# A list scheduler that counts the delay between dependent VectorE and ScalarE operations, in a fused gated-convolution forward and backward kernel

## The chip, the cores and the metric

The kernel runs on one core of a Trainium2 chip. The metric is the device time of one launch in microseconds, and a version's time is the median of its runs. The engines are TensorE (PE in the profile; PEld are its weight loads), VectorE (DVE), ScalarE (ACT), GpSimd (POOL) and SyncE (SP), which issues most of the DMAs.

## The reference, cut to what matters

The reference computes one output and nine gradients of a layer on x of shape 2048 x 512 in bf16:

```python
xn = layernorm(x)
# branch A: a short causal filter, a gate, a long causal convolution by FFT, a gate
k_shift = sum(k_pad[:, t:t+S, :] * shift_k[:, 3-t] for t in range(4))
kv = k_shift * v
y  = irfft(rfft(pad(kv)) * rfft(pad(ssm_k)))[:S] + kv * ssm_D
s  = xn * y
# branch B: gated linear unit, F = 1376
h = sigmoid(xn @ w_gate) * (xn @ w_up)
g = silu(h @ w_down)
out = x + s * g
# then the gradients of out for x, k, v, shift_k, ssm_k, ssm_D, w_gate, w_up, w_down, given grad_out
```

## The kernel before

The 2048 rows are 16 tiles of 128. The long convolution is done with matrix products against sine and cosine tables that the kernel makes itself at its start, in four channel groups of 128. The work has these stages.

*Start* (`gen_fft_consts`, `k_t`, `f_ln`, `f_xt`). Integer products of two index vectors are made (`m`), shifted into range, and turned by ScalarE's Sin into the table `Cf`; smaller tables `TB` follow. The first convolution kernel `KT` gets `ssm_D` added to its first column and is transposed on TensorE. Four small matmuls spread the short filter `skr` over the partitions, and ScalarE copies them to `skb`. The first tiles of x are normalised: `bn_stats`, `bn_aggr`, then GpSimd's power for 1/sqrt (`f_ln`), and are transposed (`f_xt`), on TensorE or by a DMA. POS is a tile's place in the order in which the tiles are taken.

*Forward* (streams `strG`, `strK`, `strV`, `strX`, interleaved). `strG` computes gate and up projections for nine tiles (`f_gen`). `strK`, `strV` and `strX` take the convolution through its steps `step1`, `flip`, `step3`, `inv3`, `inv1`. Nearly every matmul group is emptied from PSUM by ScalarE or VectorE.

*Backward* (`stepB`). For each tile: `z_gen` (down projection, silu and its derivative), `d_gen` (gradients of gate and up), `x_gen` (gradient of x through both projections and the LayerNorm). The remaining tiles' `f_gen` run in between, and from its later part the weight gradients `dW`.

*Convolution's backward* (`frontC`, `backC`, with `dW` in between), then the rest of `dW` and the drain.

The functions don't emit instructions. `Rec` records every operation with the operations it depends on, in program order (number `n`). `Rec.order` then plays the whole program through a list of costs (`cost`, `dcost`), engine by engine, and `emit` writes the instructions in the order so found; therefore nearly all instructions carry one line number, that of `emit`. In `order`, `free[e]` is the time at which engine `e` is free, `soon[e]` holds operations whose inputs have a known ready time, and `now[e]` those that are ready; of `now[e]` the one with the lowest `n` is taken. `either` holds PSUM evictions that ScalarE or VectorE may do. An operation whose input comes from the same engine counts as ready at once when the one before it has issued: `r = t + occ`, where `t` is the start and `occ` the time that the engine is held. `fin` is the time at which the result is there, some 0.085 us after `t + occ` on VectorE and 0.11 us on ScalarE. PSUM slots are given out in the same pass (`slot`), so the order also settles which eviction a matmul group waits for.

In `x_gen`, `dxn` is the gradient of the normalised x, `sm` holds two row sums, and the result is `u1 = xn * sm[3] + (dxn * r + sm[2])`, to which the direct gradient `goj` is added before it is stored.

Of the kernel before, what the change touches and what calls it, by code (L numbers as in the profile page):

```python
# [8 lines left out]
ACT = mybir.ActivationFunctionType  # L9
ALU = mybir.AluOpType  # L10
# [6 lines left out]
P = 128  # L17
# [153 lines left out]
class Rec:  # L171
# [176 lines left out]
    def order(self):  # L348
# [55 lines left out]
        while ndone < len(ops):  # L404
            best = None
            for e in self.ENGS:
                while soon[e] and soon[e][0][0] <= free[e]:
                    heapq.heappush(now[e], heapq.heappop(soon[e])[1])
                c = None
                if now[e]:  # L410
                    c = (free[e], now[e][0], e, 0)
                elif soon[e]:
                    c = (soon[e][0][0], soon[e][0][1], e, 0)
                if either and e in ("scalar", "vector"):
                    o = min(either, key=lambda o: (max(o.ready, free[e]), o.n))
                    s = (max(o.ready, free[e]), o.n, e, 1)
                    late = free["scalar"] - s[0]
                    if e == "scalar" or late > (0.4 if c is None or c[0] > s[0] + 0.6 else 1.6):
                        if c is None or s[:2] < c[:2]:
                            c = s  # L420
                if c is not None and (best is None or c[:2] < best[:2]):
                    best = c
            if best is None:
                raise RuntimeError("the order is stuck: " + str({k: len(v) for k, v in blocked.items()}))
            t, n, e, shared = best
            op = ops[n]
            if shared:
                either.remove(op)
            else:
                heapq.heappop(now[e] if now[e] else soon[e])  # L430
            q = 1 if shared and e == "vector" else 0
            new = [v for v in op.tiles if v.bank is None]
            if new:
                got = slot(new[0].kind)
                if got is None:
                    blocked[new[0].kind].append(op)
                    continue
                if got[0] > t:
                    op.ready = got[0]
                    push(op)  # L440
                    continue
                new[0].bank = got[1][0]
                for b in got[1]:
                    owner[b] = new[0]
            alt = op.alts[q]
            d = 0.0
            if op.dma:
                occ, d = self.dcost(alt)
                me, other = ("gpsimd", "hw") if e == "gpsimd" else ("hw", "gpsimd")
                t = max(t, pipe[me] - 12.0)  # L450
                t0 = max(pipe[me], t + 1.5)
                share = min(d, max(0.0, pipe[other] - t0))
                pipe[me] = t0 + d + share
                if share:
                    pipe[other] += share
                fin = pipe[me] + (DSL if t > 6 else 1.0)
            else:
                occ, lat = self.cost(alt)
                if e == "scalar" and alt[1] == "activation":
                    f = {ACT.Sin: "sin", ACT.Sigmoid: "sig"}.get(alt[2][2])  # L460
                    if f and f != table:
                        table = f
                        occ, lat = occ + 1.28, lat + 1.28
                fin = t + lat
            free[e] = t + occ
            op.done, op.fin, op.eng = True, fin, e
            seq.append((op, q, t, occ, d))
            ndone += 1
            while lo < len(ops) and ops[lo].done:
                lo += 1  # L470
            while held and held[0] <= lo + LOOK:
                o = ops[heapq.heappop(held)]
                o.ready = max(o.ready, t)
                push(o)
            for v in op.tiles:
                v.left -= 1
                v.last = max(v.last, fin)
                if v.left == 0:
                    for b in range(8):
                        if owner[b] is v:  # L480
                            owner[b] = None
                            banks[b] = v.last + 0.05 + PSL
                    for kind, lst in blocked.items():
                        for o in lst:
                            o.ready = max(o.ready, 0.0)
                            push(o)
                        lst.clear()
            for s in op.succ:
                if s < 0:
                    o = ops[~s]  # L490
                    o.wait -= 1
                    if o.wait == 0:
                        push(o)
                    continue
                o = ops[s]
                if (e == "tensor" and o.alts[0][0] == "tensor") or (e == o.alts[0][0] and len(o.alts) == 1 and not op.dma):
                    r = t + occ
                else:
                    r = fin + 0.045 + (PSL if o.alts[0][0] == "tensor" and not op.dma else 0.0)
                o.ready = max(o.ready, r)  # L500
                o.wait -= 1
                if o.wait == 0:
                    push(o)
# [38 lines left out]
def gen_fft_consts(nc, ar, negpi, Cf, TB):  # L542
# [14 lines left out]
    m = tmp([4, 4, 128], i32)  # L557
    mc = tmp([4, 2, 4, 128], i32)
    for h in range(4):
        eng = nc.gpsimd if h > 0 else nc.vector  # L560
        eng.tensor_tensor(out=m[:, h], in0=a[:, 4 * h:4 * h + 4, None].to_broadcast([P, 4, 128]),
                          in1=b[:, None, :].to_broadcast([P, 4, 128]), op=ALU.mult)
    for h in range(4):
        js = slice(4 * h, 4 * h + 4)
        if h > 1:
            yield
        nc.vector.tensor_scalar(mc[:, h, 1], m[:, h], 19, 19, ALU.logical_shift_left, ALU.arith_shift_right)
        nc.scalar.activation(Cf[:, 1, js], mc[:, h, 1], ACT.Sin, scale=-sc)
        nc.vector.scalar_tensor_tensor(mc[:, h, 0], mc[:, h, 1], -1, mc[:, h, 1], ALU.mult, ALU.max)
        nc.scalar.activation(Cf[:, 0, js], mc[:, h, 0], ACT.Sin, bias=negpi[:, 1:2], scale=-sc)  # L570
# [58 lines left out]
def kernel_impl(ctx, tc, A_q, A_k, A_v, A_shift_k, A_ssm_k, A_ssm_D, B_x, B_w_gate, B_w_up, B_w_down,  # L629
                grad_out, out_0, out_1, out_2, out_3, out_4, out_5, out_6, out_7, out_8, out_9):  # L630
    nc = tc.nc
# [81 lines left out]
        nc.scalar.activation(xnA[:, i, :], xj, ACT.Identity, bias=nmr_all[:, i:i + 1], scale=rstd_all[:, i:i + 1])  # L713

    def f_xt(i):
        if POS[i] > 1 and not 8 < POS[i] < 12:
            T[i]["xnT"] = xnT_r.next()
            nc.sync.dma_start_transpose(T[i]["xnT"], xnA[:, i, :])
            return
        pt = ps_tr([4, 128], name="ps_xnT")  # L720
        for db in range(4):
            nc.tensor.transpose(pt[:, db, :], xnA[:, i, db * 128:(db + 1) * 128], ident)
        T[i]["xnT"] = xnT_r.next()
        nc.evac(T[i]["xnT"], pt[:], 512)
# [125 lines left out]
    consts = gen_fft_consts(nc, ar, negpi, Cf, TB)  # L850
    next(consts)
    make_identity(nc, ident)
    for db in range(4):
        pb = ps_acc([512])
        nc.tensor.matmul(pb[:], ones1, skr[:, db * 512:(db + 1) * 512], start=True, stop=True)
        nc.scalar.copy(skb[:, :, db * 128:(db + 1) * 128], pb[:].rearrange("p (d t) -> p t d", t=4))
    for _ in k_t(0):
        pass
    next(consts)
    f_ln(SEQ[0])  # L860
    next(consts)
    f_xt(SEQ[0])
    f_ln(SEQ[1])
# [326 lines left out]
    def x_gen(i):  # L1190
        dgT, duT, dxa, goj, xn = T[i]["dg"], T[i]["du"], T[i]["dxa"], T[i]["go"], xnA[:, i, :]
        psX = ps_acc([D], name="psX")
        n = 0
        for srcT, wT in ((duT, wuT), (dgT, wgT)):
            for fb in range(NFB):
                nc.tensor.matmul(psX[:], srcT[:, fb, :], wT[:, fb, :], start=(n == 0), stop=(n == 2 * NFB - 1))
                n += 1
                if n % 6 == 0:
                    yield 6 * 512
        dxn, u1, sm = dxn_r.next(), u1_r.next(), small.next()  # L1200
        r = rstd_all[:, i:i + 1]
        nc.vector.scalar_tensor_tensor(dxn, psX[:], 1.0, dxa, ALU.mult, ALU.add, accum_out=sm[:, 0:1])
        nc.vector.scalar_tensor_tensor(u1, dxn, 1.0, xn, ALU.mult, ALU.mult, accum_out=sm[:, 1:2])
        nc.vector.scalar_tensor_tensor(sm[:, 2:4], sm[:, 0:2], -1.0 / D, r.to_broadcast([P, 2]), ALU.mult, ALU.mult)
        nc.scalar.activation(u1, dxn, ACT.Identity, bias=sm[:, 2:3], scale=r)
        nc.vector.scalar_tensor_tensor(u1, xn, sm[:, 3:4], u1, ALU.mult, ALU.add)
        nc.vector.tensor_tensor(goj, u1, goj, ALU.add)
        nc.gpsimd.dma_start(o1C[:, i, :], goj)
        yield 4 * 512
# [321 lines left out]
```

## Time and profile before

| | |
|---|---|
| median of 7 runs | 527.25 us (525.61 to 531.6) |
| the profiled execution's own time | 525.5 us |
| its span in the profile | 523.7 us |
| TensorE busy | 495.5 us (95%), 5429 matmuls |
| VectorE busy | 408.4 us (78%), 775 instructions |
| ScalarE busy | 332.7 us (64%), 443 instructions |
| GpSimd busy | 128.5 us (25%), 246 instructions |
| DMA | 113.19 MB, mean 216 GB/s |

In a timeline line the first two numbers are the start and the time from the first instruction's start to the last one's end, both in microseconds; then come engine, line, operation, output<-input with shapes, and the number of instructions that were merged. In brackets stands the idle time of the engine ahead of it and what ended that. In a line of waits stand the total, how often, and the longest. TensorE's matmuls overlap and their ends are modelled, so its busy time is no measure of its speed; the spacing of their starts is.

### The profile page before, as it was taken

To read this page: it belongs to the slowest core of one execution; us is meant where nothing else is said; L and a number is where in the kernel's file an instruction comes from. 1 tells how busy PE (TensorE), PEld (TensorE's weight loads), DVE (VectorE), ACT (ScalarE), POOL (GpSimd) and SP (SyncE) were. 2 spreads that over 40 slices of the span, in tenths; PEclk is the share of its full clock that TensorE was granted. 3 is DMA by queue.
4 is the path that set the end of the run, shared out by engine and by line. 5 is a ranking of instruction groups with operands and counts; after the bars stand their busy time and mean duration, and the time that the engine had idled before them with its cause. 6 is when DMAs were issued, how large, how long until landed. Compare 5 with 4: busy or idle time off the path is not lost.

```text
span 523.7 us, 13530 instructions
## 1 busy us (share of the span) xinstructions
PE 495.5 (95%) x5429; PEld 351.1 (67%) x5429; DVE 408.4 (78%) x775; ACT 332.7 (64%) x443; POOL 128.5 (25%) x246
## 2 busy tenths in 40 slices
PE   3799999999999999999999999999999999999997
PEld 2688797888886676677775556544575665775744
DVE  8879999976749889978789999635758768883754
ACT  6689999999874345344443443335878968786621
POOL 8344524454504414414153221010000000000000
PEclk9999999999999999999999999999999999999999
DMA  9989996879999754646399846999699889999884
GB/s 217 278 233 319 314 304 179 247 232 245 228 206 213 167 152 145 203 117 199 107 248 248 207 135 184 231 294 222 172 247 230 195 245 248 259 201 240 190 224 118
DMA packets 182793, 113.19 MB, mean 216 GB/s; under 512 B 132521, under 2 KB 167241, under 8 KB 182474
## 3 DMA queue, kind: packets, MB, share of 16 engines
q1 hardware_dynamic: 171096, 78.43, 63.8%
q0 software_dynamic: 11104, 33.89, 21.3%
q8 instruction: 42, 0.69, 0.6%
q14 instruction: 21, 0.17, 0.1%
q10 hardware_dynamic: 530, 0.01, 0.1%
HBM read 37.65 MB, written 45.72 MB: 159 GB/s over the span
## 4 chain that ended last, share of the span: by engine, by line
PE 53%; DVE 23%; ACT 9%; issue 7%; DMA 3%; SPq 2%; POOL 2%; DVEq 0%; POOLq 0%; ACTq 0%
PE psum L512 53%; DVE slab L512 23%; ACT slab L512 9%; SPq L512 2%; DMA slab<-in_B_w_down_dram 1%; POOL slab L512 1%; DMA slab<-in_A_k_dram 1%; POOL KK_d L512 1%; DMA slab<-slab 1%; POOL hF_d L512 0%; DVEq L512 0%; POOLq L512 0%; ACTq L512 0%; POOLq L1515 0%
## 5 line engine op out<-in xcount | busy, mean ns | idle before, releaser
L512 PE MATMUL psum<-slab 128*128 128x128 bf16 (+4 forms) x5429 | 495.5, 255 | 24.7 <-DVE slab L512 11.8
L512 PEld LDWEIGHTS <-slab 128*128 128x128 bf16 (+2 forms) x5429 | 351.1, 99 | 168.7 <-DVE slab L512 20.6
L512 DVE TENSOR_TENSOR slab<-slab 128x512 bf16<-128x512 bf16 (+5 forms) x469 | 267.2, 608 | 45.9 <-ACT slab L512 29.8
L512 ACT CAST slab<-psum 128x1024 bf16<-128x1024 f32 (+3 forms) x270 | 217.8, 847 | 101.5 <-PE psum L512 77.4
L512 ACT ACTIVATE slab<-psum 128x512 bf16<-128x512 f32 (+2 forms) x80 | 54.5, 681 | 46.1 <-PE psum L512 43.6
L512 ACT COPY slab<-psum 128x1024 bf16<-128x1024 bf16 (+1 forms) x45 | 43.0, 991 | 16.7 <-PE psum L512 16.7
L512 ACT ACTIVATE slab<-slab 128x512 bf16<-128x512 bf16 (+2 forms) x46 | 33.0, 729 | 21.9 <-DVE slab L512 21.4
L512 POOL DMA_DIRECT2D out_dram<-slab x32 | 17.5, 545 | 103.4 <-DVE slab L512 103.4
L512 DVE CAST slab<-psum 128x1024 bf16<-128x1024 f32 (+2 forms) x24 | 27.0, 1125 | 15.6 <-PE psum L512 14.9
L512 DVE TENSOR_TENSOR slab<-psum,slab 128x512 bf16<-128x512 f32 (+2 forms) x47 | 29.3, 626 | 9.7 <-ACT slab L512 6.6
L512 POOL DMA_DIRECT2D hF_d<-slab x48 | 26.0, 545 | 32.8 <-DVE slab L512 32.2
L512 POOL MEMSET slab<- 1x384 bf16 (+2 forms) x13 | 4.5, 352 | 119.3 <-PE psum L512 118.8
L512 DVE SCALAR_TENSOR_TENSOR slab<-slab 128x512 bf16<-128x512 bf16 (+3 forms) x57 | 30.6, 536 | 3.2 <-ACT slab L512 1.1
L512 DVE SCALAR_TENSOR_TENSOR slab<-psum,slab 128x512 bf16<-128x512 f32 x16 | 11.0, 688 | 21.0 <-PE psum L512 21.0
L512 POOL DMA_DIRECT2D KK_d<-slab x32 | 17.4, 546 | 27.6 <-ACT slab L512 21.4
L512 DVE TENSOR_SCALAR slab<-slab 128x1 f32<-128x1 f32 (+10 forms) x57 | 19.0, 349 | 5.5 <-POOL slab L512 3.7
L512 POOL DMA_DIRECT2D slab<-in_A_q_dram x29 | 16.0, 553 | 7.3 <-DMA out_dram<-slab 3.7
L512 DVE STREAM_TRANSPOSE slab<-slab 128x1024 f32<-128x1024 f32 x8 | 14.3, 1819 | 4.3 <-ACT slab L512 4.3
L512 POOL TENSOR_TENSOR slab<-slab 128x1 f32<-128x1 f32 (+1 forms) x19 | 13.7, 727 | 12.5 <-DVE slab L512 12.2
L512 POOL DMA_DIRECT2D slab<-hF_d x18 | 9.7, 541 | 10.3 <-PE psum L512 9.4
L512 DVE BATCH_NORM_STATS2 slab<-slab 128x6 f32<-128x512 bf16 x16 | 11.0, 685 | 0.5 <-DMA slab<-in_A_q_dram 0.5
L512 POOL DMA_DIRECT2D slab<-in_grad_out_dram x16 | 8.9, 559 | 7.4 <-DMA out_dram<-slab 4.5
(20 smaller groups left out, 33.5 us busy)
## 6 DMA issues: line engine op xcount, KB each, us to landing
KK_d<-slab POOLq DMA_DIRECT2D x32, 256.0 KB, 4.8
slab<-KK_d SPq DMA_DIRECT2D x16, 512.0 KB, 4.4
slab<-in_A_k_dram SPq DMA_DIRECT2D x8, 512.0 KB, 6.8
hF_d<-slab POOLq DMA_DIRECT2D x32, 128.0 KB, 4.3
slab<-slab SPq DMA_DIRECT2D x32, 128.0 KB, 4.2
out_dram<-slab POOLq DMA_DIRECT2D x32, 128.0 KB, 2.8
uF_d<-slab SPq DMA_DIRECT2D x32, 128.0 KB, 2.2
gF_d<-slab SPq DMA_DIRECT2D x32, 128.0 KB, 2.3
```

Of the source, the lines that this page charges most:

```text
L512: getattr(getattr(self.nc, eng), meth)(*[place(v) for v in a], **{x: place(v) for x, v in k.items()})
```

## The change

In `order`, the ready time of an operation behind another of its own engine becomes `fin + 0.034` on VectorE and ScalarE, and the choice on these two engines changes: operations that will be ready within 0.125 us are put among the ready ones, and if the lowest-numbered is one that is not ready yet, a ready one with a number less than 300 higher is taken ahead of it (a filler). The order of the whole program is made anew with this, on all engines, and with it the choice between ScalarE and VectorE for evictions and the PSUM slots.

Three further edits: the three index products that GpSimd made are made on VectorE, each ahead of the shift that reads it; the first `k_t` and `f_ln` stand ahead of the four `skb` matmuls, and the tiles at places 2 and 3 are transposed on TensorE and not by a DMA; in `x_gen` the scaled sum `xn * sm[3] + u1`, one VectorE instruction, becomes a scaling on ScalarE (into `dxn`, which nothing reads any more) and a VectorE addition.

```diff
             for e in self.ENGS:
-                while soon[e] and soon[e][0][0] <= free[e]:
+                near = 0.125 if e in ("vector", "scalar") else 0.0
+                while soon[e] and soon[e][0][0] <= free[e] + near:
                     heapq.heappush(now[e], heapq.heappop(soon[e])[1])
                 c = None
                 if now[e]:
-                    c = (free[e], now[e][0], e, 0)
+                    n0 = now[e][0]
+                    if near and ops[n0].ready > free[e]:
+                        n0 = min((n for n in now[e] if ops[n].ready <= free[e] and n < n0 + 300), default=n0)
+                    c = (max(free[e], ops[n0].ready) if near else free[e], n0, e, 0)
...
-                if (e == "tensor" and o.alts[0][0] == "tensor") or (e == o.alts[0][0] and len(o.alts) == 1 and not op.dma):
-                    r = t + occ
+                if e == o.alts[0][0] and len(o.alts) == 1 and not op.dma:
+                    r = fin + 0.034 if e in ("vector", "scalar") else t + occ
...
     for h in range(4):
-        eng = nc.gpsimd if h > 0 else nc.vector
-        eng.tensor_tensor(out=m[:, h], in0=a[:, 4 * h:4 * h + 4, None].to_broadcast([P, 4, 128]),
-                          in1=b[:, None, :].to_broadcast([P, 4, 128]), op=ALU.mult)
-    for h in range(4):
         js = slice(4 * h, 4 * h + 4)
         if h > 1:
             yield
+        nc.vector.tensor_tensor(m[:, h], a[:, 4 * h:4 * h + 4, None].to_broadcast([P, 4, 128]),
+                                b[:, None, :].to_broadcast([P, 4, 128]), ALU.mult)
...
-        if POS[i] > 1 and not 8 < POS[i] < 12:
+        if POS[i] > 3 and not 8 < POS[i] < 12:
...
     make_identity(nc, ident)
+    for _ in k_t(0):
+        pass
+    next(consts)
+    f_ln(SEQ[0])
     for db in range(4):
         pb = ps_acc([512])
         nc.tensor.matmul(pb[:], ones1, skr[:, db * 512:(db + 1) * 512], start=True, stop=True)
         nc.scalar.copy(skb[:, :, db * 128:(db + 1) * 128], pb[:].rearrange("p (d t) -> p t d", t=4))
-    for _ in k_t(0):
-        pass
-    next(consts)
-    f_ln(SEQ[0])
...
         nc.scalar.activation(u1, dxn, ACT.Identity, bias=sm[:, 2:3], scale=r)
-        nc.vector.scalar_tensor_tensor(u1, xn, sm[:, 3:4], u1, ALU.mult, ALU.add)
+        nc.scalar.activation(dxn, xn, ACT.Identity, scale=sm[:, 3:4])
+        nc.vector.tensor_tensor(u1, u1, dxn, ALU.add)
```

More of the change, by code (lines that the diff above doesn't have):

```diff
@@ L429, in order @@
             else:
-                heapq.heappop(now[e] if now[e] else soon[e])
+                if now[e]:
+                    now[e].remove(n)
+                    heapq.heapify(now[e])
+                else:
+                    heapq.heappop(soon[e])
             q = 1 if shared and e == "vector" else 0
```

## The prediction

> **What bounds the kernel now.** I read the windows by stage first, then the shape groups of TensorE, then TensorE's waits in each stage, then the timeline of the start. The windows (start and length; busy time and instructions of PE, PEld, DVE, ACT, POOL; clock; DMA) cut the span into start, forward, backward, convolution's backward, and tail:
> ```profile
> 0.00:26.00 26.00, 14.35 (x116) 11.80 (x117) 22.07 (x61) 16.41 (x23) 15.04 (x32) 1.00 0.96 248
> 26.00:145.00 119.00, 112.20 (x1738) 100.60 (x1735) 99.80 (x145) 112.30 (x135) 53.05 (x101) 1.00 0.94 255
> 145.00:355.00 210.00, 206.91 (x1977) 135.34 (x1974) 172.08 (x429) 89.75 (x157) 59.20 (x111) 1.00 0.75 191
> 355.00:503.00 148.00, 144.83 (x1510) 93.97 (x1508) 106.48 (x130) 110.14 (x122) 1.23 (x3) 1.00 0.98 224
> 503.00:523.70 20.70, 17.18 (x101) 9.43 (x98) 7.94 (x11) 4.14 (x8) 0.00 (x0) 0.99 0.51 150
> ```
> TensorE looks full, but a waiting matmul can look busy, so I price its work by spacing. Two stretches of one shape in its timeline:
> ```profile
> 107.76 6.53 PE L512 MATMUL psum<-slab 128*128 128x128 bf16 x114 [0.17 <-DVE slab L512]
> 341.80 7.50 PE L512 MATMUL psum<-slab 128*128 128x512 bf16 x34
> ```
> Less the last one's own 0.22 and 0.38 us, these are steps of (6.53-0.22)/113 = 0.056 and (7.50-0.38)/33 = 0.216 us. With the shape groups: 3916 x 0.056 = 219.3; 1060 of 512 columns x 0.216 = 229.0; 128 of 352 and 64 of 256 at 0.149 and 0.109, between the two, 26.1; the 256 small diagonal ones run four abreast, 64 x 0.07 = 4.5. That is 479 us of work in a span of 523.7. The other 45 us are all that any reordering can reach. Counting the shapes in each window gives the loss: 26 - 112 x 0.056 - 4 x 0.216 = 18.9 us in the start (3.2 of it before the first matmul), 12 in the forward, 3.6 in the backward, 6 in the last two together, and 4 from the last matmul to the end. So most of the loss is in the first quarter, and the backward, where VectorE is busiest, has almost none.
>
> TensorE's own waits: first the start, then the forward (two lines), the backward (two lines) and from 355 us on (one line):
> ```profile
> PE psum L512 <- DVE slab L512: 7.9, 4, 2.7
> ...
> PE psum L512 <- ACT slab L512: 4.3, 13, 0.8
> PE psum L512 <- DVE slab L512: 1.6, 4, 0.7
> ...
> PE psum L512 <- DVE slab L512: 2.0, 4, 0.8
> PE psum L512 <- ACT slab L512: 1.0, 1, 1.0
> ...
> PE psum L512 <- ACT slab L512: 2.7, 7, 0.6
> ```
> The start waits for VectorE; the forward is ScalarE's (112.3 busy of 119); the backward is TensorE's.
>
> **Part 1, the order.** What the new ready times can save is seen in three VectorE instructions:
> ```profile
> 200.09 0.43 DVE L512 TENSOR_TENSOR slab<-slab 128x512 bf16<-128x512 bf16 x1
> 200.45 0.75 DVE L512 SCALAR_TENSOR_TENSOR slab<-slab 128x512 bf16<-128x512 bf16 x1
> 201.24 0.43 DVE L512 TENSOR_TENSOR slab<-slab 128x512 bf16<-128x512 bf16 x1
> ```
> The second does not read the first and starts 0.07 us before its end. The third reads the second and starts 0.04 us after its end. Over all such neighbours in the trace it is -0.083 against +0.034: 0.117 us for each dependent neighbour. In the built orders I counted VectorE instructions directly behind one whose result they read: start 16 before, 2 after; forward 31 and 19; backward 182 and 44; convolution's backward 47 and 24. So 187 go, 22 us of VectorE, 16 of them in the backward.
>
> The Trainium skill ("VectorE: DVE Perf Modes", section "The DRAIN you can't avoid") speaks against this: each instruction flushes the pipe before the next, and eight copies took 13.88 us with or without semaphores between. By it the order's two terms below (-0.5 and -2.0) would be nothing, and the sum -2.3. The 0.117 above disagrees with it, and I follow the trace.
>
> In the backward the 16 us are off the path, because TensorE has other matmuls there. What can come back is what TensorE waited: 2.0 for VectorE and 1.0 for ScalarE. I take -2.0; bounds -3.0, and +1.0 if a filler delays a step that TensorE wants. In the forward VectorE gives back 12 x 0.117 = 1.4 us; of TensorE's 1.6 us of waits for it I take -0.5; bounds -1.6 and 0. From 355 us on the planner moves eight evictions of 1024 columns from VectorE (1.22 each) to ScalarE (0.90 from start to start), 7 us onto an engine with 38 us idle there. TensorE's 2.7 us of waits for ScalarE may shrink or grow: I take 0; bounds -1.5 and +2.0.
>
> **Part 2, the start.** The timeline of VectorE, then of TensorE:
> ```profile
> 2.76 1.41 DVE L512 SCALAR_TENSOR_TENSOR slab<-slab 128x512 int32<-128x512 int32 x1
> 7.43 0.69 DVE L512 SCALAR_TENSOR_TENSOR slab<-slab 128x512 int32<-128x512 int32 x1
> 8.04 0.16 DVE L512 TENSOR_TENSOR slab<-slab 128x1 bf16<-128x1 bf16 x1
> 17.84 1.22 DVE L512 CAST slab<-psum 128x1024 bf16<-128x1024 f32 x1
> ...
> 19.11 5.17 PE L512 MATMUL psum<-slab 128*128 128x128 bf16 x47 [2.67 <-DVE slab L512]
> ```
> The same instruction takes 1.41 us while GpSimd makes its three products (2.40 to 6.25) and 0.69 without. Now GpSimd loses them and VectorE gets three of 0.69, 0.61 from start to start. In the new order the add at 8.04, which TensorE's first transposes wait for, stands behind three products, two shifts (0.35) and two maxima (0.61): 1.57 + 3 x 0.61 + 2 x 0.35 + 2 x 0.61 = 5.3 us. Its operand (A_ssm_D) lands at 5.6, so it moves 2.4 us earlier. GpSimd's power for the first LayerNorm stands behind iotas alone. The whole run of table instructions, summed the same way with 14 fewer dependent neighbours, ends near 14.4 us instead of 17.9.
>
> The wait at 19.11 is for a PSUM slot that VectorE empties at 17.84 to 19.06, after its tables. In the new order ScalarE empties it, right behind its last table Sin, which now ends by 15.16; with about 1.0 us that gives 15.2 to 16.2. The up weights land at 15.6. So the first projection starts near 15.9: -3.2. Bounds: -3.5 (the landing), and -1.0, if later loads (third weight chunk, 22.1 us) or slow first matmuls take it back; 16 transposes at 8.25 take 1.93 us, 0.114 a step, twice the later 0.056, while the granted clock reads 1.00. The four skb products move behind or between the transposes; their first reader is on VectorE at 30.5 us, so that costs nothing; if that cover went, it is 0.5 us each.
>
> **Part 3, two more transposes on TensorE.** Eight of 0.056 us, and two evictions of 512 columns on ScalarE, 0.47 us from start to start. ScalarE is the bound there, and otherwise its forward count is the same (141 becomes 143): +0.9; bounds 0 and +1.8. SP loses two transposing issues (1.49 us at 30.16), and the loads behind them go sooner; no engine waits for those now.
>
> **Part 4, the x gradient.** Sixteen times a 0.78 us step on VectorE becomes one of 0.34 to 0.45, about 6 us less, and ScalarE gets 16 x 0.72 = 11.5 us. Behind the added ScalarE step stand evictions of psD and sigmoids, which free TensorE's PSUM. ScalarE is busy 90 of 210 us there, so I cost it at nothing; without that cover it is up to 11.5. The VectorE gain lies in the same covered stretch, and is in the -2.0.
>
> **The sum.** -3.2 + 0.9 - 0.5 - 2.0 + 0 = -4.8. The profiled execution took 525.5 (span 523.7 and 1.8 around it) and becomes 520.7. The median of the runs is 1.75 above it: 522.4.
>
> **Rivals.** *No change:* the start's gain is lost again before the forward's end, because ScalarE is the bound and is no lighter. Then only -2.0 or so is left, 525.3. For it: ScalarE's 94% in the forward. Against it: ScalarE itself waits for VectorE up to 17.96 and starts the forward earlier.
>
> *Slower:* fillers. A filler runs ahead of a step that is at most 0.125 us from ready, and that step then waits for all of it. The new order has 37 such fillers of 1024 columns or more (26 on VectorE, 11 on ScalarE, most after 355 us), each some 1.0 us in place of 0.12. If a third of them delay TensorE, 12 x 0.9 = 10.8, less 4.8: 533.3. It decides from about six. Against it: only 3 us of such waits are in that stage now, with weight-gradient matmuls in between.
>
> *More:* the lighter VectorE and the earlier start also take most of the 5.9 us of waits in the forward: 518.
>
> **Chances.** Forecast 0.50, more 0.10, no change 0.22, slower 0.18. A measurement of this kernel tells about 0.5%, 2.6 us, from no change. Faster 0.60, within 0.22, slower 0.18. The bounds add to -9.6 and +3.8; they will not all meet, and the slower rival lies past the upper one, so the range is 517 to 530.
>
> **What would show it.** Right: the first projection's matmuls near 16 us instead of 19.11; no 1.41 us maxima; VectorE's busy time down by 25 us or more with TensorE's unchanged; no TensorE wait for VectorE in the backward. Wrong: TensorE's waits for ScalarE after 355 us above 5 us (fillers), or the forward's end, 145 us, not moved (no change), or steps of dependent instructions that did not shrink.

## The result and the profile after

The changed kernel takes 520.67 us (median of 12 runs, 518.6 to 523.43), against 527.92 us for the kernel before (31 runs, 524.71 to 536.61): a ratio of 0.9866 [0.984, 0.9892], about 7 us faster. In a second comparison (c0 below) it was 0.9915 [0.9879, 0.9951], about 4.5 us. Runs more than 1.5% above a kernel's fastest are left out of every ratio; the profiled executions of e2, c0, g1 and f1 below are such runs, so no total is read from them.

The profiled execution of after took 522.31 us (span 520.5), high among its runs, and that of before 525.5, low among its own. The two traces therefore show 3.2 us of the 7.

The busy line of after, and its windows by stage (start, forward, backward, convolution's backward, tail; columns as in the prediction):
```profile
PE 496.5 (95%) x5437; PEld 351.4 (68%) x5437; DVE 377.3 (72%) x768; ACT 350.5 (67%) x471; POOL 127.1 (24%) x243
```
```profile
0.00:26.00 26.00, 18.32 (x199) 15.12 (x200) 21.52 (x69) 20.62 (x28) 14.03 (x34) 1.00 0.97 259
26.00:145.00 119.00, 113.06 (x1739) 101.41 (x1737) 99.01 (x148) 113.40 (x138) 52.77 (x97) 1.00 0.93 259
145.00:355.00 210.00, 206.51 (x1924) 133.63 (x1923) 157.08 (x425) 95.44 (x170) 59.08 (x110) 1.00 0.78 191
355.00:503.00 148.00, 144.68 (x1500) 93.20 (x1499) 92.32 (x123) 118.11 (x131) 1.22 (x3) 1.00 1.00 222
503.00:520.50 17.50, 13.89 (x85) 8.03 (x82) 7.35 (x6) 2.98 (x6) 0.00 (x0) 0.99 0.45 137
```
VectorE's 408.4 us became 377.3. In the first 26 us TensorE does 199 matmuls instead of 116. In the backward VectorE fell from 172.08 to 157.08, and TensorE's busy time did not rise.

TensorE's waits in after: the start (three lines), the forward (two), the backward (three), and from 355 us on (two):
```profile
PE psum L520 <- DMA slab<-in_A_shift_k_dram: 3.2, 1, 3.2
PE psum L520 <- ACT slab L520: 2.5, 3, 1.4
PE psum L520 <- DVE slab L520: 1.9, 2, 1.7
...
PE psum L520 <- ACT slab L520: 4.5, 15, 0.4
PE psum L520 <- DVE slab L520: 0.8, 2, 0.6
...
PE psum L520 <- DMA slab<-slab: 2.3, 2, 1.6
PE psum L520 <- DVE slab L520: 1.1, 1, 1.1
PE psum L520 <- ACT slab L520: 0.2, 1, 0.2
...
PE psum L520 <- ACT slab L520: 2.6, 7, 0.8
PE psum L520 <- DVE slab L520: 0.6, 1, 0.6
```
In the start the wait for VectorE fell from 7.9 to 1.9, and part of it now reads as a wait for ScalarE. In the backward the waits for VectorE and ScalarE fell from 3.0 to 1.3, and 2.3 us of waits for a DMA from slab to slab stand in their place.

To place gains and losses I priced each matmul by its spacing (0.056 us and so on, as in the prediction) and noted when TensorE had done so many us of its own work. The lead is how much earlier that is than in the profiled execution of before, in us (own working from the traces; the end is the last matmul's). For reading along: 20 lies just behind the start, 116 at the forward's end, 300 late in the backward, 400 in the convolution's backward.

| us of work done | 8 | 20 | 60 | 116 | 200 | 300 | 400 | 450 | end |
|---|---|---|---|---|---|---|---|---|---|
| after | 5.1 | 6.5 | 4.2 | 5.8 | 6.2 | 5.2 | 6.3 | 3.8 | 3.3 |
| e1, order only | 2.6 | 2.4 | -0.1 | 1.4 | 2.0 | 2.6 | 3.6 | 1.8 | 2.5 |
| e3, products on GpSimd | 2.6 | 4.3 | 1.1 | 0.6 | 1.0 | 1.2 | 2.3 | 0.4 | 0.6 |
| e4, scaled sum on VectorE | 4.9 | 6.4 | 4.1 | 6.0 | 6.8 | 7.2 | 8.3 | 6.2 | 6.4 |
| c0, after once more | 4.9 | 6.5 | 4.2 | 6.5 | 4.7 | -2.0 | -0.9 | -2.8 | -2.9 |
| f1, weights earlier | 4.3 | 6.1 | 3.4 | 2.6 | 3.0 | -3.0 | -1.9 | -3.8 | -3.6 |

After wins its time by the first 20 us of work, carries most of it through the forward and the backward, gains 1.1 us between 300 and 400 and gives back 2.5 us between 400 and 450.

The start in after, VectorE and then TensorE:
```profile
3.97 1.27 DVE L520 SCALAR_TENSOR_TENSOR slab<-slab 128x512 int32<-128x512 int32 x2
14.72 0.81 DVE L520 TENSOR_SCALAR slab<-slab 128x128 int32<-128x128 f32 x2
```
```profile
5.98 1.93 PE L520 MATMUL psum<-slab 128*128 128x128 bf16 x16 [1.75 <-DVE slab L520]
15.35 4.96 PE L520 MATMUL psum<-slab 128*128 128x128 bf16 x56 [0.90 <-ACT slab L520]
```
Two integer maxima now take 1.27 us together, where one took 1.41; the table run ends at 15.5 instead of 17.9; the first transposes start at 5.98 instead of 8.25, and the first projection at 15.35 instead of 19.11, behind an eviction on ScalarE.

### The profile page after: what moved, and what is told of

It is laid out like the page before. It is cut to its first block, busy times and chain, and to the rows that moved or that the text cites. A ratio compares the mean times of both kernels' runs of the same rounds, so it can differ in the third digit from the quotient of the medians.

```text
span 520.5 us, 13565 instructions
## 1 busy us (share of the span) xinstructions
PE 496.5 (95%) x5437; PEld 351.4 (68%) x5437; DVE 377.3 (72%) x768; ACT 350.5 (67%) x471; POOL 127.1 (24%) x243
## 4 chain that ended last, share of the span: by engine, by line
PE 64%; ACT 11%; DVE 9%; DMA 6%; issue 5%; POOL 2%; SPq 2%; ACTq 0%; DVEq 0%; POOLq 0%
PE psum L520 64%; ACT slab L520 11%; DVE slab L520 9%; DMA slab<-slab 4%; POOL slab L520 2%; SPq L520 2%; DMA out_dram<-slab 1%; DMA slab<-in_A_k_dram 0%; POOL hF_d L520 0%; ACTq L520 0%; DVEq L520 0%; POOLq L520 0%; POOLq L1522 0%
## 5 line engine op out<-in xcount | busy, mean ns | idle before, releaser
L520 DVE TENSOR_TENSOR slab<-slab 128x512 bf16<-128x512 bf16 (+6 forms) x488 | 265.5, 600 | 69.0 <-ACT slab L520 40.5
L520 ACT CAST slab<-psum 128x1024 bf16<-128x1024 f32 (+5 forms) x283 | 232.2, 879 | 85.7 <-PE psum L520 78.1
L520 ACT ACTIVATE slab<-psum 128x512 bf16<-128x512 f32 (+2 forms) x80 | 55.9, 700 | 57.1 <-PE psum L520 53.8
L520 ACT ACTIVATE slab<-slab 128x512 bf16<-128x512 bf16 (+2 forms) x62 | 44.8, 727 | 12.8 <-DVE slab L520 12.2
L520 DVE TENSOR_SCALAR slab<-slab 128x1 f32<-128x1 f32 (+10 forms) x57 | 17.2, 323 | 5.6 <-POOL slab L520 4.6
L520 POOL DMA_DIRECT2D slab<-in_A_q_dram x29 | 16.0, 552 | 19.9 <-DMA out_dram<-slab 14.4
L520 DVE SCALAR_TENSOR_TENSOR slab<-slab 128x512 bf16<-128x512 bf16 (+3 forms) x41 | 16.9, 414 | 1.6 <-POOL slab L520 1.1
L520 DVE CAST slab<-psum 128x1024 bf16<-128x1024 f32 (+1 forms) x11 | 12.4, 1124 | 5.3 <-PE psum L520 3.9
L520 POOL TENSOR_TENSOR slab<-slab 128x1 f32<-128x1 f32 x16 | 11.8, 736 | 11.7 <-DVE slab L520 11.6
```

The source lines that it names most:

```text
L520: getattr(getattr(self.nc, eng), meth)(*[place(v) for v in a], **{x: place(v) for x, v in k.items()})
```

## The experiments

### The order alone (e1), and the hand edits alone (e2)

e1 is the kernel before with the new ready times and the filler rule, none of the other edits. e2 is the changed kernel with the old rules.

```diff
 # e1, against before
+                near = 0.125 if e in ("vector", "scalar") else 0.0
...
+                    r = fin + 0.034 if e in ("vector", "scalar") else t + occ
 # e2, against after: these lines back to the old ones
```

> The version before with the new ready times and choice of fillers alone; table products on GpSimd, sum in x_gen, skb and tile transposes as before. In its order dependent VectorE neighbours are 90 (276 before), and the first step1 eviction is still on VectorE. Theory 'start' (the gain is made before 26 us, by earlier tables and that eviction on ScalarE): 525 to 528 us, the first projection still near 19 us. Theory 'order' (the gain is the shorter VectorE chains): 520 to 522 us.

> The changed version with the old ready times and choice: only the three hand edits. Dependent VectorE neighbours 288, the first step1 eviction on ScalarE. Theory 'start': 520 to 523 us, the first projection near 16 us. Theory 'order': 526 to 528 us.

e1: 522.59 us, ratio 0.9949 [0.9927, 0.9971]. Its runs lie within 522.18 to 525.2. Its busy line:
```profile
PE 494.7 (95%) x5429; PEld 351.0 (67%) x5429; DVE 384.4 (74%) x765; ACT 340.9 (65%) x453; POOL 129.0 (25%) x246
```
In the built orders dependent neighbours on VectorE went from 276 to 90. The traces follow (own working): pairs that overlap, by 0.082 us on average in both kernels, rose from 430 to 564, and gaps of 0.02 to 0.06 us, 0.034 or 0.035 on average, fell from 247 to 82. The 134 more overlaps are 11.0 us of VectorE's busy time. Another 12.7 us is work that went away, for the most part evictions: ten fewer of 1024 f32 columns (20 before, 10 in e1, at 1.22 us), and three more of the cheaper bf16 ones (6 and 9, at 0.68). Together that is nearly the 24.0 us (408.4 - 384.4) that VectorE's busy time fell. So less than half of it is the overlap itself, and most of the rest is evictions moved to ScalarE.

But 24 us of VectorE bought only 2.7 us of time by the ratio, between what the two theories had expected. By the table, 2.4 is there at 20 us of work, the forward takes 1.0 of it, the backward adds 1.2, the convolution's backward up to 400 adds 1.0, and the rest gives 1.1 back. TensorE's only wait in e1's backward is a new one, in place of 3.0 us for VectorE and ScalarE:
```profile
PE psum L520 <- DMA slab<-slab: 1.8, 2, 1.0
```

e2: 538.23 us. Five of its six runs lie 1.6% or more above the sixth, so there is no ratio; but the sixth, 528.52, is no faster than before (525.95 in that comparison), and both theories had expected less. Its start can be read:
```profile
15.29 5.33 PE L512 MATMUL psum<-slab 128*128 128x128 bf16 x56 [0.90 <-ACT slab L512]
```
With the old rules the first projection starts at 15.29, with the new rules alone (e1) at 18.00. The early projection is the hand edits' work. In the profiled execution 16.9 us were lost between 116 and 300 us of work. These two waits of TensorE are 12.6 of them, and two stretches at half the granted clock behind such waits (6.8 and 3.4 us) cost an estimated 4.5 more, half of the 9.0 us for which TensorE worked in them. Hand edits without the new order brought nothing:
```profile
PE psum L512 <- DVE slab L512: 8.9, 6, 4.7
PE psum L512 <- DMA slab<-slab: 3.7, 2, 2.7
```

### The products back on GpSimd (e3)

```diff
 # against after: as in before
+        eng = nc.gpsimd if h > 0 else nc.vector
+        eng.tensor_tensor(out=m[:, h], ...)
```

> The changed version with the three table products back on GpSimd. Theory 'start': 523 to 526 us, with maxima of 1.4 us again, the add of ssm_D near 8 us and the first projection 2 to 3 us later than in the changed version. Theory 'order': 520 to 521 us, as the changed version.

531.37 us, ratio 1.0026 [0.9977, 1.0075]: by the ratio all of the gain is gone. TensorE's timeline:
```profile
7.51 1.93 PE L520 MATMUL psum<-slab 128*128 128x128 bf16 x16 [4.29 <-DVE slab L520]
17.99 12.19 PE L520 MATMUL psum<-slab 128*128 128x128 bf16 x176 [1.72 <-DVE slab L520]
```
The first projection is back at 17.99, waiting for VectorE, and the lead at 116 is 0.6 us instead of 5.8. Its profiled execution was the quickest of its runs; why the others are up to 14 us slower is not shown.

### Only the eviction (e8)

The kernel before, with the first `step1` eviction fixed on ScalarE.

```diff
-                nc.evac(Qg[:, :, o:o + 32]..., 1024)
+                (nc.scalar.copy if stA.setdefault("s1", 0) == 0 else lambda d, s: nc.evac(d, s, 1024))(Qg[:, :, o:o + 32]..., ...)
+                stA["s1"] += 1
```

> The version before with one eviction, the first of step1, fixed on ScalarE. Theory 'start': 524 to 526 us, since the first projection no longer waits for VectorE's 19.06 us but for ScalarE near 16 to 17 us. Theory 'order': 527 to 528 us, no change, since VectorE's chains are as before.

526.03 us, ratio 0.9989 [0.9957, 1.0022]: nothing. The edit did not reach what it was made for. The two first evictions only changed places, and the first projection still waits for the one on VectorE:
```profile
17.84 1.22 DVE L512 CAST slab<-psum 128x1024 bf16<-128x1024 f32 x1
19.11 5.17 PE L512 MATMUL psum<-slab 128*128 128x128 bf16 x47 [2.68 <-DVE slab L512]
```
ScalarE's timeline tells why its eviction would come no sooner:
```profile
17.96 0.83 ACT L512 ACTIVATE slab<-slab 128x640 f32<-128x640 int32 x1 [2.80 <-DVE slab L512]
18.69 0.99 ACT L512 CAST slab<-psum 128x1024 bf16<-128x1024 f32 x1
```
ScalarE's eviction stands behind the last table Sin, which waits 2.80 us for VectorE's tables, and it ends at 19.68, later than VectorE's 19.06. That the engine does not matter while the tables are late is therefore argued from these lines; no run shows it.

### The changed kernel again (c0), with pieces undone (g1, e4) and the weights ahead (f1)

c0 is the changed kernel in a new comparison. g1 orders the convolution's backward by the old rules. e4 puts the scaled sum of `x_gen` back on VectorE. f1 loads the first third of the gate and up weights ahead of k and v.

```diff
 # g1, against after (nC: the number of operations recorded when frontC begins)
...
+                    r = fin + 0.034 if e in ("vector", "scalar") and s < self.nC else t + occ
 # e4, against after
-        nc.scalar.activation(dxn, xn, ACT.Identity, scale=sm[:, 3:4])
-        nc.vector.tensor_tensor(u1, u1, dxn, ALU.add)
+        nc.vector.scalar_tensor_tensor(u1, xn, sm[:, 3:4], u1, ALU.mult, ALU.add)
 # f1, against after: this line ahead of the loads of k and v
+    ld_w(0, 512)
```

> The changed version itself, a second profile beside the next three kernels. About 0.986 to 0.989 of the version before, 518 to 523 us. If TensorE's two waits for a transposing DMA in the backward (2.3 us in the first profile) are chance in the DMA's landing, they differ here; if they belong to the order, they stand in the same places.

> The changed version, but operations of the convolution's backward are ordered with the old ready times and without fillers; the instructions of all engines are the same up to 355 us. Theory 'late loss' (the new order costs some 2.5 us after 355 us, where eight evictions move to ScalarE and fillers stand ahead): 2 to 3 us faster than the changed version, and TensorE loses about 1 us between 440 and 480 us instead of 3.5. Rival (the new order is worth something there too): 1 to 3 us slower.

> The changed version with the scaled sum of x_gen back on VectorE as one instruction; the same instructions up to the backward. If TensorE covers the backward, as the loss of 4 us in 210 says: within 1 us of the changed version. If VectorE's 6 us there are on the path: 2 to 5 us slower.

> The changed version with the first third of the gate and up weights loaded ahead of the first k and v tiles. If the first projection (15.35 us) is held by the landing of these weights: it starts 1 to 3 us earlier, and the version is 1 to 2 us faster. If it is held by the emptying of a PSUM slot (ScalarE, 15.3 us): no earlier, within 1 us, or slower, because the filter's products on VectorE get k and v later.

| | median, us | ratio |
|---|---|---|
| c0 | 523.04 (517.88 to 529.53) | 0.9915 [0.9879, 0.9951] |
| g1 | 525.62 (519.4 to 529.9) | 0.9955 [0.9919, 0.9992] |
| e4 | 519.67 (517.09 to 521.46) | 0.9879 [0.9844, 0.9914] |
| f1 | 528.39 (520.65 to 532.56) | 0.9956 [0.9911, 1.0002] |

**e4.** Without the scaled sum on ScalarE the kernel is as fast, perhaps a little faster; the intervals overlap. The sizes were as priced: in after the 128x512 activations on ScalarE take 37.1 us in the backward against 25.2 here, and VectorE 157.08 against 162.91. They lie beside TensorE's work and move nothing.

**g1.** From 400 us of work to the end, the profiled executions took 81.7 us in before, 84.7 in after, 83.7 in c0 and 82.1 in g1. That looks like 1.6 us for the old order, but the new one had gained 1.0 of it just ahead, between 330 and 340. From 320 us of work, where 355 us on the clock stand in before, to the end it is 165.7 us in before, 167.5 in after, 166.5 in c0 and 166.0 in g1. Half a microsecond is left, and by the ratios g1 is not faster than c0.

**f1.** The weights' landing did not hold the projection: it starts at 15.86, again behind 0.90 us of waiting for an eviction on ScalarE, and the lead at 20 is 6.1 us, below after's. Later k and v cost 3 to 4 us by the forward's end (lead 2.6 instead of 5.8 and 6.5).

**c0.** This is the same program as after, and at 116 us of work it leads by 6.5. Then it loses 8.5 us up to 300. TensorE's waits in its backward, and SyncE's queue in the two executions, after first and then c0 (start and time to issue):
```profile
PE psum L520 <- DMA slab<-slab: 6.3, 1, 6.3
```
```profile
269.66 1.20 SPq L520 DMA_TRANSPOSE slab<-slab  x1
271.03 2.55 SPq L520 DMA_TRANSPOSE slab<-hF_d  x1
275.83 6.32 SPq L520 DMA_TRANSPOSE slab<-hF_d  x1
...
283.35 1.20 SPq L520 DMA_TRANSPOSE slab<-slab  x1
284.65 5.10 SPq L520 DMA_TRANSPOSE slab<-hF_d  x1
```
```profile
282.96 1.21 SPq L520 DMA_TRANSPOSE slab<-slab  x1
284.26 10.43 SPq L520 DMA_TRANSPOSE slab<-hF_d  x1
```
The slab-to-slab transposes are those of `dz` in `z_gen` (`dzT`); the ones from `hF_d` are the large transposing loads `ld_L` for the weight gradients, on the same queue. The `dzT` issued at 269.66, before those loads, landed 2.7 us later. The one at 283.35 has them around it and landed 6.3 us later, and in c0 the one at 282.96 took 12.1. TensorE's timeline, after and then c0, starts again just then:
```profile
289.73 6.52 PE L520 MATMUL psum<-slab 128*128 128x128 bf16 x65 [1.58 <-DMA slab<-slab]
```
```profile
295.09 8.12 PE L520 MATMUL psum<-slab 128*128 128x128 bf16 x64 [6.25 <-DMA slab<-slab]
```

### The late `dzT` transposed on TensorE (h1 to h4)

h1 takes the collision away: the `dzT` of tiles 9 to 12 are transposed on TensorE. h2 adds g1's edit, h3 takes the filler rule out (the new ready times stay), h4 puts the products back on GpSimd.

```diff
 # h1, against after
-        if 0 < i < NJ - 3:
+        if 0 < i < NJ - 7:
 # h3, against h1
-                near = 0.125 if e in ("vector", "scalar") else 0.0
+                near = 0.0
```

> The changed version with the dzT of tiles 9 to 12 transposed on TensorE and not by a DMA, so that none stands among the large transposing loads of the weight gradients (ld_L) on SyncE's queue. Theory 'collision' (TensorE's waits of 2 to 6 us for a transposing DMA near 290 us come from those loads, and so does the spread of the runs): TensorE waits less than 1 us for DMA in the backward, runs within some 3 us of each other, 516 to 519 us. Rival (the DMA is late for another reason, or TensorE then waits for ScalarE's evictions instead): 520 us or more, with the same spread.

> As h1_dzT_pe, and the convolution's backward ordered with the old ready times without fillers. If the new order loses there: the time from 400 us of TensorE's work to the end 1.5 to 2.5 us shorter than in h1_dzT_pe, 514 to 517 us in all. If not: the same or slower.

> As h1_dzT_pe, with the new ready times but without the 0.125 us allowance, so without fillers taken ahead of an operation that is nearly ready. If the ready times alone do the work: within 1 us of h1_dzT_pe. If the fillers do it: 2 to 4 us slower. If the fillers cost, as the slower rival of the prediction had it: 1 to 3 us faster.

> As h1_dzT_pe, with three table products back on GpSimd. Theory 'start': the first projection near 18 us instead of 15.4, and 3 to 5 us slower than h1_dzT_pe. Theory 'order': within 1 us of it.

| | median, us | ratio |
|---|---|---|
| h1 | 525.13 (521.79 to 526.09) | 0.9933 [0.9905, 0.996] |
| h2 | 526.62 (523.57 to 528.44) | 0.9955 [0.9923, 0.9988] |
| h3 | 522.92 (521.37 to 524.99) | 0.9902 [0.9863, 0.9941] |
| h4 | 531.13 (527.29 to 535.76) | 1.0044 [1.0009, 1.008] |

TensorE's waits in h1's backward:
```profile
PE psum L520 <- DVE slab L520: 2.9, 1, 2.9
PE psum L520 <- ACT slab L520: 1.4, 3, 1.0
```
The DMA wait is gone, but 2.9 us of a wait for VectorE came in its place, and h1 is not faster. Its runs lie within 4.3 us, where c0's spread over 11.7; but that was on another chip, and the changed kernel's runs in its first comparison lay within 4.8, so the collision is not shown to be what spreads them. h2 says once more that the old order late in the program brings nothing. h3 is at least as good as h1 (the intervals overlap): the fillers are worth nothing and may cost a little, which leaves the ready times as what works in the new rules. h4 against h1 is the cleanest price of the products on VectorE, on the same chip and with the late `dzT` loads out of the way: 1.0044 against 0.9933, 1.1% or some 6 us. The first projection's 2.6 us (17.99 instead of 15.35) are less than half of that. The two profiled executions, 12 us apart, stand at opposite ends of their runs and don't place the rest; in h4's, TensorE waits 2.9 us for VectorE twice, at 143.8 and at 321.8 us. Why the start's edit reaches there is not settled; the program is ordered anew with every edit.

No version was clearly faster than the changed kernel; e4 is its equal.

## Why the prediction was right

The forecast was 522.4 us, and 520.67 lies inside its range and on its side. The sum of -4.8 us stands against -3.2 between the two profiled executions, -4.5 in the second comparison and about -7 between the medians. It is in part luck that it fits, since the errors of the terms offset each other: by the leads the start brought 3.3 us more than its term, the backward 2.6 less, and the stage behind it lost 1.8. Of the signs named, the projection near 16, the maxima and VectorE's busy time (31.1 us less) came; the fourth did not, since a wait of 1.1 us for VectorE is left in the backward.

- **The start, -3.2: right in mechanism, undersized.** The projection moved from 19.11 to 15.35, 3.8 us, and the lead at 20 us of work is 6.5. The products carry the projection: undoing them takes it back to 17.99 (e3, h4), and the order alone leaves it at 18.00 (e1). What ScalarE's emptying of the slot adds is not shown, as e8 did not reach it. The leads at 20 nearly add up: 2.4 with the order alone (e1), 3.8 with the hand edits alone (e2), 6.5 with both. e3, which lacks only the products, has 4.3. The other two edits of the start, `k_t` and `f_ln` ahead of `skb` and two more tiles transposed on TensorE, were not undone by themselves. The step that was too small is that from the projection to the work behind it. I counted the projection's move and nothing else, while the transposes ahead of it also came 2.3 us earlier, and TensorE's waits up to 26 us fell from 11.7 to 7.6. Smaller misses: the table run ended at 15.5, not 14.4; ScalarE's eviction at 14.28 stands ahead of the last table Sin (15.56), not behind it; and the bound of -3.5, the landing of the up weights, was passed.
- **The forward, +0.9 - 0.5: near the mark.** The lead is 5.8 at 116 against 6.5 at 20 (4.2 between), a loss of 0.7 where 0.4 was forecast; in c0 it is 0.1. The rival "no change" had the start's gain lost by there, as ScalarE is the bound. It fell: ScalarE's 113.40 us of 119 are nearly as before (112.30), only all of it came earlier.
- **The order, -0.5 - 2.0: near the mark in size, not in place.** e1 gained 2.7 us by its ratio, but 2.4 of its lead is there by 20 us of work, the forward loses 1.0, and the backward adds 1.2 of the 2.0.
- **The backward, -2.0: wrong in the whole change.** The waits that I counted on did shrink (VectorE and ScalarE 3.0 to 1.3), but 2.3 us for `dzT` took their place: the lead is 5.8 at 116 and 5.2 at 300, a loss of 0.6, and of 8.5 in c0; only e4 shows e1's gain of 1.2. The step that failed is booking TensorE's waits for VectorE and ScalarE as gain without naming the operand that would be late next. That was `dzT`; in after it landed 6.3 us behind its issue. h1 shows that one step further VectorE is late again, with 2.9.
- **The scaled sum on ScalarE, nothing: right**, with the sizes as priced (e4).
- **After 355 us, 0: a small loss instead, inside its bounds.** From 320 us of work to the end the kernel takes 167.5 us instead of 165.7, and 165.8 to 166.5 in the five other executions with the new order on this stage (e1, e3, e4, c0, f1): a loss of 0.1 to 1.8, where the bound was +2.0. It is a gain of 1.0 up to 400 and a loss of some 2 between 400 and 450. TensorE's listed waits after 400 us on the clock don't explain that loss: 1.7 us in before, 3.2 in after, 2.2 in c0, 1.8 in g1. The evictions moved to ScalarE are a candidate; the cause is not shown.
- **The rival "slower" by fillers fell.** The waits for ScalarE that should have passed 5 us are 2.6, and h3 without fillers gains at most a little.

The prediction followed the trace's 0.117 us for a dependent pair against the Trainium skill ("VectorE: DVE Perf Modes", section "The DRAIN you can't avoid"). The overlaps and gaps counted in e1 bear the trace out. That section also says that an instruction which is not held starts earlier, which the prediction left out; so page and trace differ less than it made them. The twelve additions below run at (4.44 - 0.43) / 11 = 0.36 us from start to start, less than the 0.43 us of one:
```profile
197.83 4.44 DVE L520 TENSOR_TENSOR slab<-slab 128x512 bf16<-128x512 bf16 x12
```

## What to carry to other kernels

A scheduler that knows an engine's own delays frees much of that engine's time, 24 us here with the work that it moved elsewhere, but the kernel gets only what the bounding engine had waited for it. So price a start by when the bounding engine gets its work, and look there first for integer work that two engines do at once. Before a wait is booked as gain, name the operand that comes next and how long its transfer takes beside the traffic of that moment: here a small transpose among large loads on one queue was late in the place of the old waits, and with it moved to TensorE (h1) VectorE was late again.

## What the runs showed of the hardware

**A long wait costs more than itself.** TensorE stood still in c0 from 288.84 to 295.09 us. Its windows of 2 us (the clock is the third number from the end):
```profile
289.00:291.00 2.00, 0.00 (x0) 0.00 (x0) 0.00 (x0) 0.00 (x0) 0.00 (x0) 1.00 1.06 164
291.00:293.00 2.00, 0.00 (x0) 0.00 (x0) 0.51 (x2) 0.00 (x0) 0.00 (x0) 0.77 1.15 162
293.00:295.00 2.00, 0.00 (x0) 0.00 (x0) 1.90 (x5) 0.00 (x0) 1.56 (x5) 0.50 0.98 285
295.00:297.00 2.00, 1.91 (x19) 1.92 (x20) 1.97 (x7) 0.00 (x0) 1.25 (x3) 0.50 1.23 285
297.00:299.00 2.00, 2.00 (x19) 1.88 (x18) 1.87 (x7) 0.86 (x2) 0.00 (x0) 0.52 1.08 359
299.00:301.00 2.00, 2.00 (x21) 1.37 (x20) 0.76 (x2) 2.00 (x4) 0.54 (x1) 1.00 1.07 198
```
The granted clock fell to 0.50 some 3.2 us after the last matmul and stayed there for about 3.8 us after TensorE had begun again, so the wait of 6.25 us cost an estimated 1.9 us more. The same half clock follows the waits of 5.9 us in f1 and 4.5 in g1. Shorter waits can go either way: a wait of 2.94 us for VectorE left the clock at 1.00 in h1, the same wait of 2.94 us halved it in h2, and so did two of 2.9 in h4. In the traces behind this document every such stretch within a kernel lasts 3.41, 6.83 or 10.24 us, which are multiples of 3.41. The Trainium skill ("TensorE: Matmul & The Clock Gate", "Part 1: The HAM clock gate") states a free-running window of about 3.4 us, and half the clock after an idle one. The lengths agree, and h1 beside h2 fits a window whose phase decides. That the window must be wholly idle does not fit: the clock fell 3.25 us after the last matmul in c0 and 2.3 us after it in f1.

**Integer work without the other engine.** The maximum that took 1.41 us beside GpSimd's products takes 0.69 us without them, and 1.27 - 0.69 = 0.58 from start to start. With the products back on GpSimd (e3, h4) it takes 1.41 again. The two shifts ahead of the maxima took 1.17 us, though, where 0.7 was assumed, some 0.4 of the 1.1 us by which the tables ended later than predicted; what slowed them is not shown.
